# Low-rank token mixing after a block attention: the product over column groups of the array, without a gathering product

## The chip, the cores and the metric

The kernel runs on one core of one Trainium2 chip. The metric is the device time of that core in microseconds (us). The kernel before takes 680.86 us, the median of three executions (679.89 to 681.67). The profiled execution took 680.53 us, of which the page covers a span of 678.7 us, with a mean granted TensorE clock of 0.997.

A core has a matrix engine (TensorE, PE on the page, its weight loads PEld), a vector engine (VectorE, DVE), a scalar engine (ScalarE, ACT), a general engine (GpSimd, POOL) and a queue that issues most transfers (SyncE, SP). Products land in PSUM and are read from there by VectorE or ScalarE.

## The reference, cut to what matters

```python
# attention: 4 batches, 8 heads, 768 positions, 64 channels, in blocks of 64, with decay
intra = ((qb @ kb^T) * Dmask) @ vb
out   = intra + (qb * lam_pow) @ kv_state
kv_state = lam_block * kv_state + (kb * rev_pow)^T @ vb
# heads side by side: x is (4, 768, 512)
h = x^T @ U @ V            # U (768, 32), V (32, 768): mixing over the positions
u = x + h^T
return u + relu(u @ w_ch1) @ w_ch2     # (512, 2048) and (2048, 512)
```

The weights arrive as 64-bit floats, and the kernel takes their two 32-bit words apart itself.

## The kernel before, in words

**Tiles.** The 4 x 768 positions are 24 tiles of 128 rows, six to a batch. The attention works a tile at a time, numbered s from 0. For each tile TensorE turns q and k (`prep`, L353), makes the scores (`scores`, L398), applies the state (`inter`, L439), multiplies masked scores by v (`intra`, L451) and makes the next state's addition (`state`, L416). ScalarE copies the transposes (L356) and the result x (L456) out of PSUM and scales the old state (`fade`, L390). VectorE masks the scores (L407) and adds up the state (L422, L424). GpSimd scales q and k (L381, L370).

**Order.** The order is written out by hand in the list `pieces`. Each engine executes what is meant for it strictly in that order, so an instruction that waits holds all that come after it on its engine. Step s prepares tile s + 1 and finishes tile s. Seven tiles behind, `mix` adds the low-rank part to x (PE L497, DVE L500) and `turn` transposes the sum for the channel products (L514 and after) and writes it out (L517).

**Low-rank part.** Once per batch, h is made in two halves: p = U^T x, of 32 rows and 512 columns, by `low`, and then V^T p by `mix`. Before the change `low` gives each of the first four position tiles a column group of 32 columns of the array, so that four partial sums of p lie one below the other in PSUM (L465). The last two tiles are cut into halves of 256 columns and added to the four (L474). ScalarE copies this out (L479), and `low_sum` multiplies it by a matrix `gather` of ones and noughts (L483), which adds the four parts and writes p four times, once to each group of 32 partitions. Then p is cut into a high part, of which ScalarE writes 64 rows (L489), and a low part, of which VectorE writes 64 rows (L490). `mix` multiplies these 128 rows by v_hl, which holds V cut up to match.

**Weight conversion beside it.** `aside(s)` runs small steps out of a table: the fetches of a weight tile, then `one` (L153, L154, and two ScalarE steps L159 and L160), `two` (L170), `three` (L178), `four` (L183), `five` (L201) and so on. Tile 0 of the first channel weight is fetched in four parts in steps 3 to 6, and `one` comes in step 7. In steps 0 to 6 `aside` stands at the end of a step, from step 7 on it stands in the middle, ahead of the masking of the next tile. U is converted in steps 1 and 2, V in steps 3 to 5.

**Buffers.** There are nine tiles of x (`x_pool`), three raw tiles of q and of v and four of k, two banks pair `px` and `pss`, and single banks by tags such as "pq", "pk", "pt" and "pu". A tag's next tile waits until the last reader of the former is done.

**After the attention** come `hidden` (L708, L718), the first channel product, and then the second (L839, L841, L843). The last tiles of the attention's turning and mixing, and the last batch's low-rank part, are spread among the first products by the list `rest`.

**Start.** `keep_busy` multiplies blank tiles so that TensorE isn't idle before the first data. `constants` makes the mask by scans over the decay factors (L299), and `powers` the decay powers for q (L312).

Of the kernel before, what the change touches and what calls it, by code (L numbers as in the profile page):

```python
# [8 lines left out]
FP32 = mybir.dt.float32  # L9
# [5 lines left out]
P = 128  # L15
# [3 lines left out]
def kernel(  # L19
# [223 lines left out]
    def one_bank(shape, name, tag):  # L243
        return psf.tile(shape, FP32, tag=tag, name=name)
# [4 lines left out]
    def bank(shape, name, tag):  # L249
        return psa[0].tile(shape, FP32, tag=tag, bufs=2, name=name)  # L250
# [31 lines left out]

    gather = keep.tile([P, G, R], FP32, name="gather")
# [11 lines left out]
    def constants():  # L295
        for a in range(HP):
            for x in range(2):
                h = 2 * a + x
                nc.vector.tensor_tensor_scan(  # L299
                    mask[:, x, a, :], lamb[:, h : h + 1].broadcast_to([P, P]), ident, 0.0,  # L300
                    ALU.mult, ALU.add,
                )
        nc.vector.tensor_copy(out=rev, in_=mask[:, :, :, P - 1])
# [12 lines left out]

    def make_gather():
        grid = ident.rearrange("p (g r) -> p r g", r=R)
        nc.vector.tensor_reduce(out=gather[:, 0, :], in_=grid, axis=mybir.AxisListType.X, op=ALU.add)
        for g in range(1, G):  # L320
            nc.vector.tensor_copy(out=gather[:, g, :], in_=gather[:, 0, :])
# [137 lines left out]
    pts = {}  # L459

    def low(b):

        pp = one_bank([P, C], "pp", "pu") if b < B - 1 else bank([P, C], "pp", "b2")
        for c in range(G):
            nc.tensor.matmul(  # L465
                out=pp[c * R : (c + 1) * R, :], lhsT=u_w[:, c, :], rhs=xs[b * NT + c],
                start=True, stop=False,
            )

        n = C // 2  # L470
        assert 2 * (NT - G) == G
        for i in range(G):
            c, cols = G + i // 2, slice(i % 2 * n, (i % 2 + 1) * n)
            nc.tensor.matmul(  # L474
                out=pp[i * R : (i + 1) * R, cols], lhsT=u_w[:, c, :],
                rhs=xs[b * NT + c][:, cols], start=False, stop=True,
            )
        pts[b] = tmp("pt")
        nc.scalar.copy(pts[b], pp)  # L479

    def low_sum(b):
        pr = one_bank([P, C], "pr", "pt") if b < B - 1 else bank([P, C], "pr", "b2")
        nc.tensor.matmul(  # L483
            out=pr, lhsT=gather.rearrange("p g r -> p (g r)"), rhs=pts.pop(b),
            start=True, stop=True,
        )
        t = tmp("pt_h")
        nc.vector.tensor_scalar(t.bitcast(U32), pr.bitcast(U32), HI, None, ALU.bitwise_and)
        nc.scalar.copy(p_hl[0 : P // 2], t[0 : P // 2])  # L489
        nc.vector.tensor_tensor(  # L490
            out=p_hl[P // 2 : P], in0=pr[P // 2 : P], in1=t[P // 2 : P], op=ALU.subtract
        )
# [52 lines left out]
    pieces += [("powers", 0)]  # L545
    for s in range(NS):
# [3 lines left out]
        step = [("low", b - 1)] * (c == 0 and b > 0)  # L550
        step += [("prep", s + 1), ("scale", s + 1)] * more
        step += [("mix", done)] * (0 <= done < NS - NT - 1)
        step += [("low_sum", b - 1)] * (c == 0 and b > 0)
# [10 lines left out]
    def load_next(name, engine=nc.sync):  # L564
# [7 lines left out]
        "low": low, "low_sum": low_sum, "mix": mix, "turn": turn,  # L572
# [45 lines left out]
    for steps, at in (  # L618
        (u_side, (-1, 1, 1, 2, 2)),
        (v_steps(), (0, 0, 3, 3, 4, 4, 5, 5, 5, 5)),  # L620
        (w1_steps(0, True), (3, 4, 5, 6, 7, 8, 9, 10, 12, 13, 14)),
# [33 lines left out]
    make_gather()  # L655
    keep_busy(2)
    pl = one_bank([P, H], "pl", "pt")
    nc.tensor.matmul(out=pl, lhsT=lam_row[:, H:], rhs=lam_row[:, 0:H], start=True, stop=True)
    keep_busy(3)
    nc.vector.tensor_copy(out=lamb, in_=pl)  # L660
    constants()
    scale_k(0)
    run.update(aside=aside, late=on_scalar_late, powers=lambda s: powers())
# [89 lines left out]
    def run_units(units, side, every=lambda i: None):  # L753
# [10 lines left out]
        (0, 4, "turn", c0 - 2), (0, 6, "mix", c0 - 1), (0, 9, "low", b), (0, 14, "low_sum", b),  # L764
# [177 lines left out]
```

## Time and profile before

| view | value |
|---|---|
| median of three | 680.86 us |
| span of the profile | 678.7 us |
| PE busy | 668.4 us (98%) |
| VectorE busy | 495.8 us (73%) |
| ScalarE busy | 291.5 us (43%) |
| GpSimd busy | 114.6 us (17%) |
| share of PE in the chain that ended last | 97% |
| attention, up to its last tile | to 126 us |

The page puts the busy time of each engine beside its share of the span. The chain of work that ended last is followed back from the last instruction, at each step to what released it. A busy engine with a large share of that chain bounds the kernel; where another engine or a transfer stands in the chain, the bound changes for that stretch. The list of waits says who waited for whom, with the sum in us, the number of waits and the longest. A timeline line has the start in us, the length in us, the engine, the line of the code, the operation, output and inputs, and the number of instructions merged. Most of the attention's time passes at one step per tile, which is read between the starts of successive `px` products in the chain: 81.99, 86.73, 91.46 and 96.20 us, so 4.74 us each.

### The profile page before, as it was taken

To read this page: it belongs to the slowest core of one execution; us is meant where nothing else is said; L and a number is where in the kernel's file an instruction comes from. 1 tells how busy PE (TensorE), PEld (TensorE's weight loads), DVE (VectorE), ACT (ScalarE), POOL (GpSimd) and SP (SyncE) were. 2 spreads that over 40 slices of the span, in tenths; PEclk is the share of its full clock that TensorE was granted. 3 is DMA by queue.
4 is the path that set the end of the run, shared out by engine and by line. 5 is a ranking of instruction groups with operands and counts; after the bars stand their busy time and mean duration, and the time that the engine had idled before them with its cause. 6 is when DMAs were issued, how large, how long until landed. Compare 5 with 4: busy or idle time off the path is not lost.

```text
span 678.7 us, 13340 instructions
## 1 busy us (share of the span) xinstructions
PE 668.4 (98%) x5196; PEld 543.0 (80%) x5196; DVE 495.8 (73%) x857; ACT 291.5 (43%) x543; POOL 114.6 (17%) x92
## 2 busy tenths in 40 slices
PE   8979999999999999999999999999999999999997
PEld 7869888778888888888888888888888888888886
DVE  5658899686999777777798255787586676865854
ACT  4657777545665444444465131232232322322320
POOL 4446667331000000000000000030030210300300
PEclk9998999999999999999999999999999999999999
DMA  9898985145677655555566999955363353453421
GB/s 214 196 224 217 223 220 144 64 168 173 234 249 261 233 202 202 205 204 204 204 249 248 330 320 370 312 164 167 95 214 101 108 196 102 152 163 94 158 92 62
DMA packets 131776, 131.29 MB, mean 193 GB/s; under 512 B 81346, under 2 KB 89794, under 8 KB 131714
## 3 DMA queue, kind: packets, MB, share of 16 engines
q1 hardware_dynamic: 130656, 130.18, 60.4%
q8 instruction: 41, 0.67, 0.4%
q10 hardware_dynamic: 1058, 0.26, 0.2%
q14 instruction: 21, 0.17, 0.1%
HBM read 80.09 MB, written 50.33 MB: 192 GB/s over the span
## 4 chain that ended last, share of the span: by engine, by line
PE 97%; DVE 1%; DMA 1%; issue 0%; POOL 0%; SPq 0%; ACT 0%; DVEq 0%; POOLq 0%
PE pz L708 27%; PE pz L841 13%; PE pz L839 13%; PE pd L718 13%; PE pd L843 13%; PE px L451 4%; PE pss L398 4%; PE put L514 2%; PE pq L353 2%; PE pk L353 1%; PE px L439 1%; PE pkv L416 1%; PE pu L497 1%; DMA words<-in_moe_w_ch_dram 1%; PE pp L465 1%; PE pr L483 1%
## 5 line engine op out<-in xcount | busy, mean ns | idle before, releaser
L708 PE MATMUL pz<-u_hl,w 128*128 128x512 f32 x768 | 191.2, 398 | 0.2 <-ACT r L714 0.2
L708 PEld LDWEIGHTS pz<-u_hl,w 128*128 128x128 f32 x768 | 143.9, 188 | 36.4 <-issue 1.1
L839 PE MATMUL pz<-w_hl,m 128*128 128x512 f32 x384 | 151.6, 396 | 0.0
L841 PE MATMUL pz<-w_hl,m 128*128 128x512 f32 x384 | 151.6, 396 | 0.0
L843 PE MATMUL pd<-w_d,m 128*128 128x512 f32 x384 | 150.0, 396 | 0.0
L822 ACT ACTIVATE m<-mt 128x512 fp32r<-128x512 f32 x96 | 60.7, 632 | 195.5 <-PE pd L843 145.6
L823 DVE SCALAR_TENSOR_TENSOR m<-rm,m 128x512 fp32r<-128x512 f32 x96 | 71.5, 746 | 53.9 <-ACT m L822 53.6
L868 POOL TENSOR_TENSOR o<-o,u 128x512 f32<-128x512 f32 x20 | 29.8, 1524 | 447.5 <-DVE o L864 447.5
L723 DVE SCALAR_TENSOR_TENSOR r<-pd,r 128x512 f32<-128x512 f32 x96 | 61.8, 685 | 55.6 <-ACT r L714 41.2
L718 PE MATMUL pd<-u_d,w 128*128 128x512 f32 x384 | 98.2, 397 | 0.0
L841 PEld LDWEIGHTS pz<-w_hl,m 128*128 128x128 f32 x384 | 72.3, 188 | 17.7
L843 PEld LDWEIGHTS pd<-w_d,m 128*128 128x128 f32 x384 | 72.3, 188 | 17.6
L839 PEld LDWEIGHTS pz<-w_hl,m 128*128 128x128 f32 x384 | 72.3, 188 | 17.6
L718 PEld LDWEIGHTS pd<-u_d,w 128*128 128x128 f32 x384 | 72.2, 188 | 17.4
L714 ACT ACTIVATE r<-pz 128x512 f32<-128x512 f32 x96 | 52.0, 593 | 59.0 <-PE pz L708 59.0
L824 DVE SCALAR_TENSOR_TENSOR m<-m 128x512 fp32r<-128x512 f32 x96 | 69.0, 720 | 0.9
L821 DVE TENSOR_SCALAR mt<-rm 128x512 uint32<-128x512 uint32 x96 | 46.2, 481 | 25.8 <-DMA rm<-r_d 25.2
L204 ACT CAST w<-wt 128x512 fp32r<-128x512 f32 x32 | 19.9, 622 | 40.9 <-DVE wt L201 33.7
L407 DVE TENSOR_TENSOR sm<-pss,mask 128x512 f32<-128x512 f32 x48 | 30.8, 682 | 8.6 <-PE pss L398 8.6
L451 PEld LDWEIGHTS px<-vraw,sm 128*64 128x64 f32 x768 | 24.6, 138 | 11.2 <-DVE sm L407 6.4
L451 PE MATMUL px<-vraw,sm 128*64 128x64 f32 x768 | 28.2, 225 | 4.0 <-DVE sm L407 3.9
L381 POOL TENSOR_TENSOR qs<-qt,powq 128x512 f32<-128x512 f32 x20 | 25.8, 1289 | 25.5 <-ACT qt L356 17.2
(88 smaller groups left out, 703.6 us busy)
## 6 DMA issues: line engine op xcount, KB each, us to landing
r_d<-r SPq DMA_DIRECT2D x96, 256.0 KB, 2.4
rm<-r_d SPq DMA_DIRECT2D x96, 256.0 KB, 2.7
words<-in_moe_w_ch_dram SPq DMA_DIRECT2D x30, 512.0 KB, 4.4
w_d<-w SPq DMA_DIRECT2D x16, 768.0 KB, 3.3
w_hl<-w_d SPq DMA_DIRECT2D x16, 512.0 KB, 6.6
vraw<-in_v_dram SPq DMA_DIRECT2D x24, 256.0 KB, 4.1
u_d<-x_nat SPq DMA_DIRECT2D x24, 256.0 KB, 3.6
u<-u_d SPq DMA_DIRECT2D x24, 256.0 KB, 4.0
```

What stands on the lines that cost most here:

```text
L451: nc.tensor.matmul(out=px[half[t], x, a, :], lhsT=sm[:, x, a, half[t]], rhs=vr[:, 2 * a + x, :], start=(first and a == 0), stop=(a == HP - 1),
L708: nc.tensor.matmul(out=acc[g][0], lhsT=w[:, n, ct, :], rhs=uhl[g][:, n, ct, :], start=(ct == 0 and n == 0), stop=(ct == CT - 1 and n == 1),)
L714: nc.scalar.mul(rs[g], acc[g][0], 1.0 + E)
L718: nc.tensor.matmul(out=acc[g][1], lhsT=w[:, 2, ct, :], rhs=ud[g][:, ct, :], start=(ct == 0), stop=(ct == CT - 1),)
L723: nc.vector.scalar_tensor_tensor(rs[g], acc[g][1], 4096.0, rs[g], ALU.mult, ALU.add)
L821: nc.vector.tensor_scalar(t.bitcast(U32), r.bitcast(U32), HI, None, ALU.bitwise_and)
L822: nc.scalar.activation(out=m[:, 0], in_=t, func=AF.Relu)
L823: nc.vector.scalar_tensor_tensor(m[:, 1], r, 0.0, hi, ALU.max, ALU.subtract)
L824: nc.vector.scalar_tensor_tensor(m[:, 2], hi, E, low, ALU.mult, ALU.subtract)
L839: nc.tensor.matmul(out=pz, lhsT=m[:, 0, cols], rhs=hl[:, 0], start=first, stop=False)
L841: nc.tensor.matmul(out=pz, lhsT=m[:, 1, cols], rhs=hl[:, 1], start=False, stop=end)
L843: nc.tensor.matmul(out=pd, lhsT=m[:, 2, cols], rhs=dd, start=first, stop=end)
```

## The change

The change has four parts. `low` gives each column group of the array a quarter of the columns of x rather than a position tile of its own: for each of the six tiles, four products of 32 rows by 128 columns, which add up over the tiles in place. No sum over groups is then left, so `gather`, its product, the ScalarE copy ahead of it and its set-up go. p lies in PSUM as four blocks; `low_rows` puts them side by side with small VectorE instructions, and ScalarE twice and GpSimd once write the copies. `low` moves behind `prep` and `mix` of its step. `one` of weight tile 0, and `two`, `three`, `four` with it, come a step later. At the start two of five blank products go, `powers` moves from behind the first masking to ahead of the first scaling of k, and `rev` is copied after it.

```diff
-        pp = one_bank([P, C], "pp", "pu") if b < B - 1 else bank([P, C], "pp", "b2")
-        for c in range(G):
-            nc.tensor.matmul(
-                out=pp[c * R : (c + 1) * R, :], lhsT=u_w[:, c, :], rhs=xs[b * NT + c],
-                start=True, stop=False,
-            )
...
-        pts[b] = tmp("pt")
-        nc.scalar.copy(pts[b], pp)
-
-    def low_sum(b):
...
+        pp = one_bank([P, P], "pp", "pq") if b < B - 1 else bank([P, P], "pp", "b2")
+        for c in range(NT):
+            for g in range(G):
+                nc.tensor.matmul(
+                    out=pp[g * R : (g + 1) * R, :], lhsT=u_w[:, c, :],
+                    rhs=xs[b * NT + c][:, g * P : (g + 1) * P],
+                    start=(c == 0), stop=(c == NT - 1),
+                )
+        pps[b] = pp
+
+    def low_rows(b):
+
+        pp, t = pps.pop(b), tmp("p_h")[0:R]
+        h, h2, l, l2 = (p_hl[g * R : (g + 1) * R] for g in range(G))
+        own = [(slice(g * R, (g + 1) * R), slice(g * P, (g + 1) * P)) for g in range(G)]
+        for rows, cols in own:
+            nc.vector.tensor_scalar(
+                t[:, cols].bitcast(U32), pp[rows].bitcast(U32), HI, None, ALU.bitwise_and
+            )
+        nc.scalar.copy(h, t)
+        nc.scalar.copy(h2, t)
+        for rows, cols in own:
+            nc.vector.tensor_tensor(
+                out=l[:, cols], in0=pp[rows], in1=t[:, cols], op=ALU.subtract
+            )
+        nc.gpsimd.tensor_copy(out=l2, in_=l.bitcast(FP32))
...
-        step = [("low", b - 1)] * (c == 0 and b > 0)
-        step += [("prep", s + 1), ("scale", s + 1)] * more
+        step = [("prep", s + 1), ("scale", s + 1)] * more
         step += [("mix", done)] * (0 <= done < NS - NT - 1)
-        step += [("low_sum", b - 1)] * (c == 0 and b > 0)
+        step += [("low", b - 1)] * (c == 0 and b > 0)
+        step += [("low_rows", b - 1)] * (c == 0 and b > 0)
...
-        (w1_steps(0, True), (3, 4, 5, 6, 7, 8, 9, 10, 12, 13, 14)),
+        (w1_steps(0, True), (3, 4, 5, 6, 8, 9, 10, 11, 12, 13, 14)),
...
     make_identity(nc, ident)
-    make_gather()
-    keep_busy(2)
+    keep_busy(1)
     pl = one_bank([P, H], "pl", "pt")
     nc.tensor.matmul(out=pl, lhsT=lam_row[:, H:], rhs=lam_row[:, 0:H], start=True, stop=True)
-    keep_busy(3)
+    keep_busy(2)
     nc.vector.tensor_copy(out=lamb, in_=pl)
     constants()
+    powers()
+    nc.vector.tensor_copy(out=rev, in_=mask[:, :, :, P - 1])
     scale_k(0)
...
-        (0, 4, "turn", c0 - 2), (0, 6, "mix", c0 - 1), (0, 9, "low", b), (0, 14, "low_sum", b),
+        (0, 4, "turn", c0 - 2), (0, 6, "mix", c0 - 1), (0, 9, "low", b), (0, 14, "low_rows", b),
```

The list `pieces` also loses its own entry for `powers`.

## The prediction

> **What bounds the kernel.** I read the page first. PE is busy for 668.4 of 678.7 us and is 97% of the chain that ended last, so what the change is worth is what it takes off PE's time line. That is read from the chain in order of time (start us, length us, what):
>
> ```profile
> 9.51 1.38 DVE powq L312 x4
> 11.06 1.25 POOL qs L381
> 12.35 0.69 PE px L439 x32
> ...
> 41.41 1.08 PE px L451 x32
> 42.50 0.59 PE pkv L416 x16
> 43.09 1.02 SPq L267
> 44.16 4.31 DMA words<-in_moe_w_ch_dram
> 49.26 1.21 DVE sm L407 x2
> 50.51 1.04 PE px L451 x28
> 51.55 0.71 PE pkv L416 x16
> 52.26 1.92 PE pss L398 x32
> 54.17 0.85 PE px L439 x32
> ...
> 68.90 1.00 PE pp L465 x8
> ...
> 71.66 0.86 PE pr L483 x2
> ```
>
> Two places aren't PE: the start, and the hole from 43 to 50 us, where the last fetched part of weight tile 0 stands in the chain. The waits up to 260 us and up to 160 us say who stood there (us in total, times, longest):
>
> ```profile
> PE px L451 <- DVE sm L407: 3.9, 2, 3.6
> ```
> ```profile
> DVE sc L153 <- DMA words<-in_moe_w_ch_dram: 4.9, 1, 4.9
> ```
>
> So `one` waits at the head of VectorE's queue for a transfer that lands at 48.5 us (issued 44.16, 4.3 us to landing), the masking of tile 8 is queued behind it, and PE waits for the masking. The table by stretches (PE, PEld, DVE, ACT, POOL busy, granted clock, DMA share, GB/s) shows the aftermath:
>
> ```profile
> 43.00:51.00 8.00, 4.13 (x101) 3.61 (x99) 2.92 (x6) 2.27 (x7) 2.48 (x3) 1.00 0.92 218
> 51.00:56.00 5.00, 5.00 (x109) 4.76 (x104) 4.61 (x8) 3.92 (x9) 2.75 (x2) 0.66 0.93 240
> 77.00:96.00 19.00, 19.00 (x502) 17.45 (x500) 18.09 (x30) 15.92 (x37) 15.38 (x12) 1.00 0.90 225
> ```
>
> PE worked 4.13 of 8 us and then ran at clock 0.66. In the ordinary stretch PE is full, but VectorE is busy for 18.1 of 19 us and the DMA engines for 0.90: both stand close behind PE.
>
> **What the Trainium skill says.** *TensorE: Matmul & The Clock Gate*, "What's actually happening": after an idle window of about 3.4 us the array falls to half its clock and needs such a window of work to get back. The trace agrees: after the 3.6 us wait the scores took 1.92 us against 1.03. *TensorEngine Tiling (Array Packing)*, "Key Properties": the four 128x32 tiles load and multiply in parallel. The trace agrees: eight L465 products of 604 ns each are over in 1.06 us. *GPSIMD Engine Reference*, "Specifications": GpSimd shares its SBUF interfaces with VectorE, and two-input or two-port VectorE instructions contend. The trace fits: L201 took 0.99 us at 74.57 beside GpSimd work, 0.43 in the median.
>
> **1. `one` a step later.** The hole: `px` starts at 41.41 and, two tiles on, at 56.73, 15.32 us; two ordinary steps are 9.47. It costs 5.85 us, the wait and the slow clock together. After the change `one` stands in step 8. VectorE reached it at 43.6 us and will reach the new place an ordinary step later, at about 48.3; the part lands at 48.5, if SP keeps its times (its issues there run some 4 us behind the program because the DMA engines are full, not because PE is late). The wait is some 0.2 us. Behind it stands the masking of tile 9, with 0.5 us to spare before PE wants it. I take 5.8 us of gain; bounds 4.5 and 5.85.
>
> Moved with it: `two`, `three` and `four` to steps 9 to 11. VectorE's ordinary step is masking 1.29, turning 1.36, mixing 0.68, state 0.42, so 3.75 us, and the largest of these conversions 1.29 (L170): 5.04 against 4.74, 0.3 over for a single step, absorbed in the next. Nothing.
>
> **2. The start.** The chain runs powq, qs, then the first state product at 12.35. `powers` (1.75 us from 9.14 to 10.89) moves to before the first masking, where VectorE waited 2.06 us for the scores. k's scaling starts 1.7 us later, and ends 8.6 instead of 7.0 for tile 0, wanted by PE at 10.1: hidden. qs of tile 1 then waits for GpSimd's second scaling, at about 9.7, and ends at 11.0; the product is then free after the scores, at 11.8. With 0.3 us from fewer blanks (first q lands at 3.1, PE turned it at 4.48) this is 0.5 to 0.8 us early. But v of tile 4, issued at 22.53, lands at 26.26, and its product starts at 26.60: of the gain 0.34 gets through. I take 0.3; bounds 0 and 0.6.
>
> **3. The low-rank product on PE.** Before, from first L465 to the next transpose: 68.83 to 70.26, 1.43 us, and `pr` 0.86 in the chain. New: 24 products, 48 records as an fp32 product has two, four groups at once, so 12 rounds of 128 columns. The nearest row is L398, four small tiles at once with 128 columns: 32 records in 1.03, so 0.129 a round, and 1.55 us. From L465's 0.43 per 512 columns it would be 0.108 a round plus 0.2 of drain, 1.5. The weight loads, four in 0.13 us at L474, just keep up. PE saves 1.43 + 0.86 - 1.55 = 0.74 us a batch, and 0.1 more where a change of shape is saved. Bounds: 1.5 and, with loads and products in turn, 12 x 0.26 = 3.1.
>
> **4. `low_rows` beside it.** It takes eight VectorE instructions of 32x128 from PSUM. Rows: 256 columns 0.42, 512 columns 0.69, so 0.29 for 128; successive ones overlap by 0.06, so 0.23, 1.85 us in all. *VectorE: DVE Perf Modes*, "The TRN2 errata", gives 120 + 128 cycles, an estimate of 0.26. Against two instructions of 0.69 this is 0.45 more, in three of 24 steps. ScalarE: two casts of about 0.6 (L489 0.62) against a copy and a cast, equal, but both now stand ahead of the copy of x (L456), and `inter` of the next tile wants that bank. By batch:
> - Steps 12 and 18. `low` ends at 71.67; four ANDs to 72.7; the casts to 73.95; x to 74.5. PE wants `inter` at 74.25: 0.3 lost of 0.85. 0.5 gained each.
> - Step 6. V's conversion is in the way: VectorE is in it until 36.5, ScalarE writes V's copies for 2.08 us (L599), both ahead of the first `mix`. Following them: ANDs 37.4, casts 38.6, x 39.15, V's copies 41.15, `mix` 41.2 against 40.9 before. Also `low` waits some 0.4 us for the "pq" bank it now shares. 0.3 us lost; bounds -0.8 and +0.5.
> - Last batch, among the channel products: nothing there waits on x, `mix` is 13 instructions away. 0.75 gained.
> GpSimd's copy (L370, two inputs, takes 1.06 for 512) ends at about 75, `mix` wants it at 76.5: hidden.
>
> **5. What the DMA engines ask back.** A step moves q, k, v and the written sum, 1.05 MB, and 0.13 of weights in steps 8 to 11: 1.18 MB, 4.9 us at the highest rate seen, 240 GB/s, against 4.74. In the hole SP caught up its 4 us; now it won't. q, k, v have 8 us to spare. The nine x tiles have less: tile s takes the buffer of s - 9, whose write is issued at the end of step s - 2. From there to the copy are 6.9 us, and landing takes about 4: at 4 us behind, x is 1 us late, 0.75 us of which hides behind `state` and `scores`. I take 0.6 us in all; bounds 0 and 3.
>
> **Sum.** 5.8 + 0.3 + 0.5 + 0.5 - 0.3 + 0.75 - 0.6 = 6.95 us. Behind 126 us PE is full to the end, so it comes through: 680.86 - 6.95 = **673.9 us**.
>
> **Rivals.**
> - *The DMA engines take the hole's place.* For it: share 0.92 to 0.95 from 30 to 56 us. Against: buffers for three tiles. Half the hole comes back: 5.85/2 less, so 676.8.
> - *The row work holds PE.* For it: VectorE and ScalarE are nearly full in steps 12 and 18. Against: they had 0.7 us of idle time there. Each batch loses 0.5 instead of its gain (1.45 in sum): 3.45 us less, 677.4.
> - *Slower: the column groups don't overlap.* 48 records in turn at 0.129 are 6.2 us instead of 2.29: 3.9 us x 4 lost, 15.6, against 6.1 of points 1 and 2: 690.4. Against it: L465 overlaps by four.
>
> **Chances.** Forecast 0.66 (672.6 to 675.2), DMA 0.18, row work 0.09, slower 0.05, nothing gained 0.02. The range takes in the first two and part of the third: 672.3 to 677.2. The bound of 0.3% is 2.04 us, 678.8: faster 0.91, same 0.04, slower 0.05.
>
> **What would show it.** The wait of L153 for words falls from 4.9 us to under 0.6, with no stretch at clock 0.66; PE is busy for nearly all of 43 to 51 us. The 48 low records of a batch span about 1.55 us. In step 12 `inter` waits for ScalarE. Tile 1's `px` L439 starts before 12 us. I am wrong if `one` waits again, if ScalarE's copies of x wait for transfers by several us, or if the low records span over 3 us.

## The result, and the profile after

The changed kernel took 679.79 us in the median of four executions (679.27 to 680.83), beside 680.38 us for the kernel before (679.10 to 681.67). The ratio is 0.9993, with a 95% interval from 0.9970 to 1.0017. So the forecast of 673.9 us missed: a gain of 6.95 us was expected, and 0.5 us was measured, which can't be told from none.

Yet the wait that was to go has gone. The page says so first, in its shares of busy time and in the shares of the chain that ended last:

```profile
PE 666.0 (98%) x5312; PEld 544.2 (80%) x5312; DVE 499.2 (74%) x877; ACT 291.7 (43%) x543; POOL 116.4 (17%) x96
...
PE 93%; ACT 2%; DVE 1%; issue 1%; DMA 1%; POOL 0%; SPq 0%; ACTq 0%; DVEq 0%
```

No wait of L153 for `words` is left in the list of waits. But PE's share of the chain fell from 97% to 93%: other engines took its place on the path. The table by stretches has the same windows as before the change (PE, PEld, DVE, ACT, POOL busy, granted clock, DMA share, GB/s):

```profile
43.00:51.00 8.00, 6.82 (x169) 5.73 (x170) 4.29 (x7) 4.95 (x15) 3.38 (x3) 1.00 0.96 229
51.00:56.00 5.00, 4.52 (x113) 3.91 (x109) 4.52 (x6) 3.60 (x9) 3.91 (x4) 1.00 0.92 238
77.00:96.00 19.00, 18.36 (x491) 16.96 (x486) 16.83 (x28) 15.11 (x36) 14.77 (x12) 1.00 0.84 208
```

In the stretch of the hole PE is busy for 6.82 us instead of 4.13, and the clock stays at 1.00. But the third window was full before, 19.00 of 19, and has lost 0.64. The chain in order of time shows who stands in these places (start us, length us, what):

```profile
39.40 0.62 ACT vp L473
40.04 0.62 ACT vp L474
40.68 0.58 ACT x_nat L447
41.68 0.51 ACT vp L585
...
42.77 0.49 issue
43.51 0.81 ACT faded L381 x3
...
45.33 0.69 PE pkv L407 x16
...
51.82 0.97 DVE sc L153
52.79 1.42 DVE m L154
54.21 1.21 DVE sm L398 x2
55.46 1.06 PE px L442 x28
...
58.17 0.63 ACT sc L159
58.82 0.72 ACT sc L160
...
61.50 0.69 PE pkv L407 x16
...
84.04 0.64 issue
84.68 0.57 PE px L430 x23
```

Four things are to be seen. Around 40 us ScalarE's casts of the row work and V's copies hold the fading, and with it PE. At 52 us `one` is on the path without waiting for anything: L153 and L154 alone take 2.39 us ahead of the masking. At 58 us its exponents (L159, L160) stand on ScalarE ahead of the copies that PE wants. And at 84 us PE stops for 0.64 us with no wait at all.

A plainer measure is used below: the length of a step, from the start of the intra product of one tile to that of the next, read from the trace of each kernel. An ordinary step is 4.74 us. Step 8 is the one that ends with the product of tile 8. (The program's step s runs on past the product of tile s, so what it does last lies in the table's step s + 1.) "px 23" is when tile 23's product starts, counted from the start of the span, and "rest" is from there to the end. These are single executions, so sizes are taken from the ratios of many runs, and places from here. They differ from their start on: the product of tile 5 begins at 30.80 us before, at 32.45 after, and between 29.8 and 33.5 us in all traces, so a late tile 23 isn't by itself a loss of the edit. (The rows of e3, e5, e13, e14 and e16 are left out.)

```
step                7     8     9    10    11    12    13    14    18    19    px 23   rest
before             5.11  8.57  6.74  4.74  4.73  6.32  4.73  4.74  6.32  4.74  125.21  553.49
after              5.86  6.48  5.12  5.25  5.19  5.39  5.80  4.74  5.39  5.88  125.77  553.03
e0_before_again    5.01  7.48  5.25  5.19  4.97  6.32  4.74  4.73  6.32  4.74  124.81  553.49
e1_shift           4.38  5.58  5.19  5.26  5.18  6.32  4.74  4.73  6.32  4.74  121.02  553.48
e2_shift_low       5.84  5.88  5.12  5.25  5.18  5.39  5.80  4.74  5.39  5.95  124.01  552.79
e4_low             5.25  5.88  4.74  5.36  4.84  5.39  5.80  4.74  5.39  5.95  125.00  552.80
e6_rows_split      5.37  5.87  5.12  5.26  5.19  5.39  4.78  5.35  5.39  5.74  123.87  552.83
e7_spread          4.84  5.88  4.74  4.73  5.10  6.33  4.73  4.74  6.72  4.74  121.61  553.49
e10_split_spread   5.36  5.87  5.15  5.11  5.74  6.89  5.05  5.08  6.66  5.20  126.28  552.82
e8_before_three_v  4.30  5.50  4.74  5.23  4.97  6.32  4.74  4.73  6.32  4.73  121.68  553.32
e9_shift_three_v   4.37  5.58  5.18  5.26  5.19  6.32  4.74  4.73  6.32  4.73  121.39  553.31
e11_after_three_v  5.85  5.87  5.13  5.26  5.18  5.39  5.99  4.74  5.39  5.80  121.97  552.83
e12_split_three_v  5.37  5.87  5.13  5.26  5.18  5.39  4.78  5.08  5.39  5.05  120.38  552.62
e15_spread_three_v 5.04  5.87  4.73  4.94  4.93  5.39  5.05  5.08  6.65  5.05  122.06  552.64
```

(Steps 12 and 18 hold the low-rank product, and with it are longer than the ordinary one. Step 8 isn't an ordinary one either: in the sixteen traces without the hole, the changed kernel's aside, it takes 5.50 to 5.94 us.)

### The profile page after: what moved, and what is told of

It reads as the page before. It is cut to its first block, busy times and chain, and to the rows that moved or that the text cites. A ratio compares the mean times of both kernels' runs of the same rounds, so it can differ in the third digit from the quotient of the medians.

```text
span 678.8 us, 13604 instructions
## 1 busy us (share of the span) xinstructions
PE 666.0 (98%) x5312; PEld 544.2 (80%) x5312; DVE 499.2 (74%) x877; ACT 291.7 (43%) x543; POOL 116.4 (17%) x96
## 4 chain that ended last, share of the span: by engine, by line
PE 93%; ACT 2%; DVE 1%; issue 1%; DMA 1%; POOL 0%; SPq 0%; ACTq 0%; DVEq 0%
PE pz L695 27%; PE pz L826 13%; PE pz L828 13%; PE pd L705 13%; PE pd L830 13%; PE pss L389 3%; PE px L442 3%; PE put L501 2%; PE pq L344 1%; PE pk L344 1%; PE px L430 1%; PE pkv L407 1%; PE pp L457 1%; PE pu L484 1%; DMA kraw<-in_k_dram 1%
## 5 line engine op out<-in xcount | busy, mean ns | idle before, releaser
L389 PE MATMUL pss<-qt,kt 64*64 64x128 f32 x768 | 28.6, 282 | 1.1 <-issue 1.1
L159 ACT ACTIVATE sc<-sc,ends 128x512 f32<-128x512 uint32 x30 | 21.7, 722 | 18.4 <-DVE sc L153 18.4
```

What stands on the lines that cost most here:

```text
L389: nc.tensor.matmul(out=pss[half[t], x, a, :], lhsT=kt[half[x], a, half[t]], rhs=qt[half[x], a, :], start=True, stop=True,)
```

## The experiments

Every kernel was run beside the kernel before, in five groups on four chips. The median of the kernel before was 677.94 us in group a, 679.40 in b, 679.83 in c, 678.65 in d and 679.66 in e, so the table has ratios. Within a group they compare directly. Across groups the kernel before alone moved by 0.28%, and no run shows that another kernel moves with it; so where two groups are compared the difference of the medians in us stands beside that of the ratios, and what the two don't agree on isn't shown.

| kernel | what it is | group | median us | ratio to before | 95% interval |
|---|---|---|---|---|---|
| after | the changed kernel | own | 679.79 | 0.9993 | 0.9970 to 1.0017 |
| e0_before_again | the kernel before, unchanged | b | 680.00 | 1.0000 | 0.9980 to 1.0020 |
| e1_shift | before + later conversion | a | 677.18 | 0.9985 | 0.9969 to 1.0001 |
| e3_shift_start | e1 + the new start | a | 677.63 | 0.9986 | 0.9972 to 1.0000 |
| e4_low | before + new low-rank part | a | 678.51 | 0.9998 | 0.9975 to 1.0020 |
| e2_shift_low | e1 + new low-rank part | a | 678.56 | 1.0008 | 0.9987 to 1.0028 |
| e5_five_blanks | after + all five blanks | b | 678.44 | 0.9986 | 0.9974 to 0.9998 |
| e6_rows_split | e2 with the row work split | b | 676.94 | 0.9953 | 0.9937 to 0.9968 |
| e7_spread | conversion two steps later | b | 676.96 | 0.9964 | 0.9950 to 0.9978 |
| e8_before_three_v | before, v fetched for 3 tiles | c | 676.09 | 0.9942 | 0.9922 to 0.9962 |
| e9_shift_three_v | e1, v fetched for 3 tiles | c | 676.58 | 0.9946 | 0.9926 to 0.9966 |
| e11_after_three_v | after, v fetched for 3 tiles | d | 677.94 | 0.9986 | 0.9968 to 1.0004 |
| e12_split_three_v | e6, v fetched for 3 tiles | d | 675.51 | 0.9957 | 0.9941 to 0.9974 |
| e10_split_spread | e6 and e7 together | c | 678.93 | 0.9984 | 0.9973 to 0.9995 |
| e15_spread_three_v | e10, v fetched for 3 tiles | e | 676.34 | 0.9938 | 0.9914 to 0.9962 |
| e16_later_fetch | e10, tile 1's parts fetched later | e | 679.22 | 0.9991 | 0.9976 to 1.0005 |
| e13_spread_pt | e10, product in another bank | d | 678.98 | 1.0003 | 0.9988 to 1.0019 |
| e14_split_pt | e6, product in another bank | d | 679.58 | 1.0007 | 0.9994 to 1.0021 |

### The parts alone: conversion, start, low-rank product

**e1_shift**, the conversion alone:

```diff
-        (w1_steps(0, True), (3, 4, 5, 6, 7, 8, 9, 10, 12, 13, 14)),
+        (w1_steps(0, True), (3, 4, 5, 6, 8, 9, 10, 11, 12, 13, 14)),
```

> The kernel before with the conversion of weight tile 0 a step later, and nothing else. Theory A (each part does what it does alone, and the later step is worth nearly the whole hole at 43 us, while the row work and the colder array at the start give it back): 4.0 to 5.8 us faster than the kernel before, that is 674.6 to 676.4. Theory B (the hole was the DMA engines' rest; taken away, what it hid comes out as waits for late loads and late instructions): 1 to 3 us faster, 677.4 to 679.4, with PE idle spread over the steps after 50 us.

Measured: 0.9985, so 1.0 us of gain (0 to 2.1, hardly to be told from none), where the hole alone was to give 5.8. Step 8 is 5.58 instead of 8.57. But steps 8 to 11 sum to 21.21 us, 2.25 over four ordinary ones. Of these 0.84 are step 8's, which is over at 46.27 us, before `one` begins. The other 1.41 lie in steps 9 to 11. VectorE's instructions in order of time show the first part of them (start us, length us, what, idle before):

```profile
48.35 1.03 DVE L153 TENSOR_SCALAR sc<-words 128x512 uint32<-128x512 uint32 x1
49.30 1.50 DVE L154 TENSOR_SCALAR m<-words 128x512 uint32<-128x512 uint32 x1
50.73 1.27 DVE L407 TENSOR_TENSOR sm<-pss,mask 128x512 f32<-128x512 f32 x2
51.92 0.68 DVE L519 TENSOR_SCALAR ut<-put 128x512 uint32<-128x512 uint32 x1
```

`one` finds its words there: no idle time stands in brackets. It takes 2.38 us from 48.35 to 50.73, and the masking behind it is late. From there the chain of e1 goes through ScalarE, where the exponents (54.76 to 56.13 us) stand ahead of the copies of q and k. PE's waits from 40 to 66 us name the masking and the copy of k:

```profile
PE pkv L416 <- ACT kt L356: 0.8, 2, 0.6
PE px L451 <- DVE sm L407: 0.6, 2, 0.4
```

Of the 0.8 us for the copy of k, 0.6 are at 42 us, in step 8 and ahead of `one`; 0.2 are at 58 us, behind the exponents.

**e3_shift_start** adds the new start to it:

```diff
-    keep_busy(2)
+    keep_busy(1)
...
-    keep_busy(3)
+    keep_busy(2)
...
+    powers()
+    nc.vector.tensor_copy(out=rev, in_=mask[:, :, :, P - 1])
     scale_k(0)
```

> The changed kernel with the low-rank part as before, its gathering product included. Theory A: the row work loses 0.3, 0.1 and 0.1 us in the first three batches and gains 0.76 in the last, so it comes out even, 679.4 to 680.2. My prediction's sizes (0.5 gained in two batches, 0.75 in the last, 0.3 lost in one) would make this 1.45 us slower than the changed kernel, 681.2.

Measured: 0.9986 beside 0.9985. The start gave nothing and cost nothing that can be told.

**e4_low**, the new low-rank part alone (product, row work, order of the steps, no gathering product), and **e2_shift_low**, with the later conversion as well (e4 with the diff of e1):

> The kernel before with the new low-rank part alone. The hole at 43 us ends when the weight part lands, whatever PE lost ahead of it, so the first batch's loss is hidden in both theories. Theory A: 0.76 gained in the last batch, 0.1 lost in each of the two in between: 0.5 us faster than before, 679.9. The prediction's sizes: 1.75 us faster, 678.6.

> The changed kernel with the start as before (five blank products, the powers behind the first masking). Theory A: the start costs 1.0 to 1.7 us in the changed kernel, so this takes 678.1 to 678.8 against its 679.8. Theory B: the loads set the pace up to 30 us whatever the start does, so within 0.4 us of the changed kernel.

Measured: 0.9998 and 1.0008. In e4's trace the product of tile 7 starts at 44.27 us, 2.97 later than before, and yet that of tile 8 starts at 50.15, within 0.28 us of the 49.87 of before. Most of the 2.97 isn't the low-rank part's, as tile 5, ahead of it, was 2.67 late already. But it shows what the hole does: when PE comes late, the part has landed (L153 waits 0.2 us for it and not 4.9, and PE doesn't wait for the masking), so what goes wrong ahead of it costs next to nothing. In e2 the hole is gone, and nothing takes up the loss of steps 6 and 7. Ratio by ratio the low-rank part cost 0.0023 (1.6 us) on top of e1, 1.4 us between the medians; the two intervals overlap.

### The start again, and the kernel before again

**e0_before_again** changes nothing.

> The kernel before, unchanged, for a second profile. Theory C (the hole's end is set by when the DMA engines deliver the last part of weight tile 0, and that differs between executions by several us; the profile I predicted from showed a long one): the part is issued nearer to 42 than to 44 us, the hole between the px products of tiles 7 and 9 costs 2 to 4 us over two ordinary steps rather than 5.85, and the span is shorter by the same. Theory A (the hole is a fixed property of the program): 5.5 to 6 us again. Its time against itself shows what a comparison of this kernel can tell: 1.000 within 0.0015.

Measured: 1.0000. Its trace holds a smaller hole:

```profile
DVE sc L153 <- DMA words<-in_moe_w_ch_dram: 3.8, 1, 3.8
```

3.8 us instead of 4.9; PE stood idle for 2.62 us, not 3.61, and no slow clock followed, so step 9 is 5.25 and not 6.74. Steps 8 and 9 are 12.73 us, so the hole costs 3.26 us here and cost 5.84 in the first trace. Tile 8's product starts at 49.88 and 49.87 us in the two, although tile 7's starts are 1.10 us apart: the end of the hole stands fast, as L153 begins when the part has landed, at 48.48 and 48.50 us.

How often the long hole comes can be estimated from the mean granted clock of each execution. It was 0.997 in the trace of before, with its stretch at 0.66, and 0.999 in this one. Of the 225 executions of the kernel before in the five groups, 79 have 0.997 or less, and these take 2.1 to 2.7 us longer than the others of their group (medians). Of the 200 executions of the ten kernels with a later conversion and all of v, three have. So the slow clock seems to follow the hole in about a third of the executions. The other 44 of the kernel before in group a have a median of 677.52 us, beside 677.18 for e1: by the medians about half of what e1 gains is that this slow clock no longer comes.

**e5_five_blanks** is the changed kernel with `keep_busy(2)` and `keep_busy(3)` as before.

> The changed kernel with the five blank products of the kernel before, its powers still ahead of the first scaling. If the missing blanks leave the array at its low clock up to 10 us: scores of tile 0 back from 1.99 us to some 1.5, transposes of tile 1 from 1.1 to 0.66, and px of tile 0 about 1.0 us earlier, of which at most 0.4 us is left in the time, since v of tile 4 sets a floor at 26 us: 679.4 to 679.8 against the changed kernel's 679.8 of its own comparison. If the loads alone set the early pace: no change in the slope, and px of tile 0 within 0.2 us.

Measured: 0.9986, beside 0.9993 for the changed kernel itself, whose interval holds it. In its trace the scores of tile 0 take 1.59 us (1.99 in the changed kernel); but with five blanks as well they took 1.50 in the trace of before, 1.98 in e0_before_again and 1.99 in e1_shift. So the clock at the start differs between executions of one kernel, and the blanks aren't shown to decide it.

### Row work and conversion mended

**e6_rows_split** takes e2_shift_low and splits `low_rows`, so that the copy of x stands ahead of the casts on ScalarE, and the state's addition ahead of the subtractions on VectorE:

```diff
-        step += [("low_rows", b - 1)] * (c == 0 and b > 0)
-        step += [("intra", s)] + [("late", s)] * (done < 0) + [("state", s)]
+        new = c == 0 and b > 0
+        step += [("rows_and", b - 1)] * new + [("intra", s)] + [("rows_high", b - 1)] * new
+        step += [("late", s)] * (done < 0) + [("state", s)] + [("rows_low", b - 1)] * new
```

> The kernel with the later conversion and the new low-rank part, start as before, but with the row work taken apart: the four ANDs first, then the copy of x ahead of ScalarE's two casts, and the addition of the state ahead of VectorE's four subtractions. If the row work holds PE by standing ahead of these two: the step of tile 13 and 19 falls from 5.80 and 5.95 to 4.8 to 5.1, that of tile 7 by 0.5, and the kernel becomes 1.5 to 2.2 us faster than with the row work in one piece (678.6), 676.4 to 677.1. If something else holds PE there (GpSimd's scaling, the mode change of the array): less than 0.4 us.

Measured: 0.9953 (0.9937 to 0.9968), 3.2 us under before. In its own group it is 0.0033 under e5, the changed kernel with five blanks (1.5 us between the medians); under e2_shift_low, in another group, it is 0.0055 by the ratios and 1.6 us by the medians. So it is faster than the kernel before and than the changed one. The lines show why. ScalarE in the changed kernel, step 12:

```profile
72.22 0.62 ACT L473 CAST vp<-p_h 32x512 fp32r<-32x512 f32 x1 [2.54 <-DVE p_h L470]
72.85 0.62 ACT L474 CAST vp<-p_h 32x512 fp32r<-32x512 f32 x1
73.49 0.58 ACT L447 COPY x_nat<-px 128x512 f32<-128x512 f32 x1
```

The copy of x waits behind two casts, which waited 2.54 us for VectorE. `inter` wants the bank that this copy frees. PE's line for it:

```profile
74.18 0.69 PE L430 MATMUL px<-kv,qs 64*64 64x64 f32 x32 [0.83 <-POOL vp L479]
```

The profile puts the 0.83 us down to GpSimd's L479. But `inter` starts 0.11 us after the copy of x ends (73.49 + 0.58), it needs nothing of L479, and with the order turned round the wait is gone: step 13 falls from 5.80 to 4.78. It was the copy. (The trace of e6 as a whole doesn't show the gain: it lost 1.7 us to stops without a wait, see e12, and took 678.47 us, 1.5 over its median.)

**e7_spread** is the kernel before with the conversion of tile 0 two steps later, and that of tile 1 one step later:

```diff
-        (w1_steps(0, True), (3, 4, 5, 6, 7, 8, 9, 10, 12, 13, 14)),
-        (w1_steps(1, True), (8, 9, 10, 11, 15, 16, 17, 18, 19, 20, 21)),
+        (w1_steps(0, True), (3, 4, 5, 6, 9, 10, 11, 12, 13, 14, 15)),
+        (w1_steps(1, True), (8, 9, 10, 11, 16, 17, 18, 19, 20, 21, 22)),
```

> The kernel before with the conversion of weight tile 0 two steps later instead of one (steps 9 to 15), and tile 1's one step later (16 to 22), so that one conversion step falls in each step. If the 2.25 us that came back in the steps of tiles 8 to 11 are VectorE's and ScalarE's backlog from the conversion (L153 and L154 took 2.4 us beside GpSimd, the exponents 1.4 us on ScalarE): the later place, where the backlog of V's copies is gone, gives 0.7 to 1.3 us of it back, 675.9 to 676.5 against 677.2 with one step. If the DMA engines set the pace of these steps: no change, 677.2.

Measured: 0.9964 (0.9950 to 0.9978), 2.4 us under before. VectorE's lines for `one`:

```profile
54.27 0.43 DVE L153 TENSOR_SCALAR sc<-words 128x512 uint32<-128x512 uint32 x1
54.62 0.41 DVE L154 TENSOR_SCALAR m<-words 128x512 uint32<-128x512 uint32 x1
```

L153 and L154 take 0.43 and 0.41 us here, and 1.03 and 1.50 in e1_shift, and steps 9 and 10 are ordinary ones again. So their time depends on where they stand. GpSimd's lines beside them, in e1 and in e7:

```profile
48.04 1.06 POOL L370 TENSOR_TENSOR ks<-kraw,small 128x512 f32<-128x512 f32 x1 [0.32 <-POOL qs L381]
49.05 1.46 POOL L536 TENSOR_TENSOR u_d<-te,u_hl 128x512 fp32r<-128x512 f32 x1
```

```profile
54.58 1.59 POOL L536 TENSOR_TENSOR u_d<-te,u_hl 128x512 fp32r<-128x512 f32 x1 [0.95 <-ACT te L534]
```

In e1 L153 ends 0.28 us after the first of them, and L154 0.29 us after the second. The other traces agree. In the twelve in which GpSimd's scaling of k was running when L153 began, L153 took 0.78 to 1.03 us and ended 0.28 to 0.29 us after it. In six (before, e7, e10, e13, e15, e16) nothing ran on GpSimd when L153 began; there the two took 0.41 to 0.44 us each, although in four of them GpSimd's u_d ran beside L154. So an instruction of GpSimd that is there first seems to hold VectorE's until it is done, rather than both being slowed. This fits the shared SBUF interfaces that the prediction names; it is read from the order of the times, as no run took GpSimd's work away.

### The transfers taken away

Five kernels (e15 further down) fetch v for their first three tiles only, and leave out the fetches of the other 21:

```diff
+        if name == "v" and s >= 3:
+            raw[s, name] = kept[s % 3]
+            return
...
+        if name == "v":
+            kept[s] = t
```

> The kernel before, but v is fetched for the first three tiles only and those three buffers are used again for all later tiles (the output is not the reference's). A tile then moves a quarter less, some 0.79 instead of 1.05 MB, in the same time. Theory A (the hole is the DMA engines' backlog: the weight part is issued 4 us late because the engines are full): the part is issued when the program asks for it, L153 doesn't wait for it, the step of tile 8 falls from 8.57 us (before) or 7.48 (the same kernel again) to under 5.3, tile 9's too, and the run is 3.3 to 5.8 us shorter than before: ratio 0.991 to 0.995. The gaps that PE shows with no wait, once in some 253 records, become shorter as well. Theory B (the part is issued late because SP or the program's order holds it, not the engines): L153 still waits 3 us or more and the ratio is within 0.998 to 1.002.

**e8** measured 0.9942 (0.9922 to 0.9962), 3.9 us under before, with no wait for `words` in its list, while `one` is still in step 7. Step 8 is 5.50, where under 5.3 was expected. So the hole was the backlog of the transfers and not the place of `one`. The edit both lightens the DMA engines and takes v's issues off SP's queue, where they took 2.1 to 2.7 us each from 37 to 48 us in the trace of before; it doesn't part the two.

> The same cut of v's transfers, on the kernel with the later conversion alone (the output is not the reference's). If the 2.25 us that tiles 8 to 11 lose there are the conversion's own (VectorE beside GpSimd, ScalarE's exponents) and not the transfers', the steps of tiles 8 to 11 stay at 5.2 to 5.6 us, so that this kernel gains only 0 to 2 us on the same kernel with all of v, and ends beside or behind the kernel before with v cut: ratio 0.992 to 0.998. If the full DMA engines cause them, these steps fall to 4.75, and it is some 2.2 us faster than with all of v: ratio 0.993 to 0.996, with the steps telling the two apart.

**e9** measured 0.9946, the same as e8: where there is no hole, moving `one` is worth nothing. And its steps 8 to 11 are 5.58, 5.18, 5.26 and 5.19, those of e1 with all of v to 0.01 us. What the conversion loses at its new place is its own and not the transfers'. (Beside e1, in another group, e9 is 0.0039 ahead by the ratios but 0.6 us by the medians, and the steps show no place for a gain.)

> The changed kernel, with v fetched for its first three tiles only (the output is not the reference's). Theory A (the loss with the new low-rank part is the engines' own: row work ahead of the copy of x, the conversion beside GpSimd): tiles 12 to 14 and 18 to 20 keep what they lose, tiles 8 to 11 too, and the kernel ends behind the one before with v cut (0.9942): ratio 0.994 to 0.998. Theory B (the transfers take it: late k at the start, late instructions, late x): the forecast's gains appear, 1.4 us below the kernel with the later conversion and v cut (0.9946): ratio 0.990 to 0.993.

**e11** measured 0.9986, just beyond the upper end of theory A and far from theory B: with the transfers out of the way the changed kernel is still behind e9, which has the old low-rank part and start, by 0.0040 (2.7 us) in the ratios and 1.4 us in the medians of the two groups. PE's waits from 60 to 126 us are one line, the copy of x again under GpSimd's name, in steps 13 and 19:

```profile
PE px L435 <- POOL vp L484: 1.7, 2, 0.8
```

> The kernel with the row work split and the start of before, with v fetched for its first three tiles only (the output is not the reference's). Without the transfers' load the gaps of PE that show no wait (0.54, 0.26 and 0.74 us in tiles 14 to 19 with all of v) should go, if a full DMA engine delays what PE fetches: then these steps fall to 4.74 and the ratio is 0.991 to 0.993. If they stay, they belong to the number of PE's instructions and not to the load: ratio about 0.995.

**e12** measured 0.9957, 2.0 us under e11 in the same group, so the split row work pays without the transfers' load as well. On the gaps without a wait it is half an answer. In the trace of e6_rows_split they are all that PE waited for from 60 to 126 us:

```profile
PE px L431 <- issue: 1.7, 4, 0.7
```

In e12's trace there is no such line, nor in those of e8, e9, e11 and e15 for that stretch. So with lighter transfers the gaps go. What they cost in a typical execution of e6 stays open: the ratio is no better (0.9957 beside 0.9953), the median is 1.4 us lower in another group, and the traced execution of e6 took 678.47 us, where its median is 676.94.

### Both repairs together

**e10_split_spread** is e6 with the conversion of e7.

> The changed kernel with the start of before, the row work split around the copy of x and the state addition, and the conversion another step later (steps 9 to 12; tile 1's 16 to 18 and so on). If the two repairs act on separate losses they add: the split was worth 0.0055 of the time against the same kernel without it, the spread 0.0021 against the kernel with the conversion one step later alone. So 0.9953 - 0.0021: ratio 0.993 (0.9915 to 0.9945), 4.8 us under before. If both only make room for the same wait (VectorE's and ScalarE's backlog in steps 8 to 12), the ratio stays at 0.9953. The steps of tiles 9 and 10 should be at 4.8, that of tile 13 under 5.

Measured: 0.9984. The repairs don't add; together they are worth less than each alone, by 0.0031 and 0.0020 in the ratios and 2.0 us in the medians. ScalarE's copies of x in steps 9, 10 and 11 tell of a wait that was in neither kernel (in brackets the idle time before, and its releaser):

```profile
54.92 0.59 ACT L448 COPY x_nat<-px 128x512 f32<-128x512 f32 x1 [1.54 <-DMA u_d<-x_nat]
60.67 0.59 ACT L448 COPY x_nat<-px 128x512 f32<-128x512 f32 x1 [2.17 <-DMA u_d<-x_nat]
66.95 0.59 ACT L448 COPY x_nat<-px 128x512 f32<-128x512 f32 x1 [2.32 <-PE pq L345]
```

A copy of x has to wait until the tile nine before has been written out of the same buffer. The writes were issued at 49.49, 55.43 and 61.29 us, and writes landed up to 5.4 us after issue in this stretch. That reaches to the first two copies. The third, which the profile puts down to PE though its product had been running since 63.67, would fit as well; the landing of its write isn't in the trace. Behind the copy on ScalarE stands that of q, and the low-rank product takes the bank that q's copy frees:

```profile
69.11 1.08 PE L458 MATMUL pp<-x_nat,u_w 128*32 128x128 f32 x32 [1.57 <-ACT qt L348]
```

> The kernel with both repairs, with v fetched for its first three tiles only (the output is not the reference's). If the transfers made the repairs cancel, ScalarE's copies of x no longer wait for the writes of x (1.5, 2.2 and 2.3 us), the low product no longer waits for the bank of q (1.57 and 0.85), tiles 12 and 18 fall to 5.4 us and tile 23 starts by 131.5 us (137.81 with all of v): ratio 0.991 to 0.995, ahead of the split alone with v cut (0.9957). If ScalarE and VectorE are out of time by themselves, the waits for the bank stay and the ratio is 0.997 to 0.999.

(That text counts tile 23 from the trace's own start, 11.2 to 11.5 us ahead of the span: 131.5 there is 120.3 here, and 137.81 is 126.28.)

**e15** measured 0.9938 (0.9914 to 0.9962). The copies of x wait for their products alone, and step 12 is 5.39. So the late copies of x were the transfers' doing. That they are all that made the repairs cancel isn't shown. Beside the split alone with v cut, e12 in another group, e15 is ahead by the ratios (0.9938 and 0.9957) but 0.8 us behind by the medians, and its tile 23 starts at 122.06 and not at 120.3, where e12's starts at 120.38. The second wait for q's bank, 0.85 us in step 18, stays with v cut, so that one isn't the transfers'.

> The kernel with both repairs, where the four parts of weight tile 1 are fetched in steps 12 to 15 and not 8 to 11, so that the writes of x no longer stand behind a part on SP's queue and a step moves 1.05 instead of 1.18 MB there. If the late writes of x made the repairs cancel, the copies of x in steps 9 to 11 wait for the products alone and the ratio is 0.993 to 0.996. If not, it stays at 0.998. A risk: the last part now lands for a conversion one step later, in step 16, where the hole of before could come back (3 us): ratio then 1.0.

**e16** moves tile 1's four fetches from steps 8 to 11 to steps 12 to 15. In its trace the copies of x no longer wait for writes, and step 12 is 5.39. But the ratio is 0.9991 (0.9976 to 1.0005): a miss, 0.0053 behind e15 in the same group. The waits of the copies can go without a gain. `one` of tile 1 waited 0.5 us for its words, step 17 grew to 5.83, and its executions lie between 676.75 and 682.97 us; the traced one took 677.90. What the slower ones wait for isn't in a trace. It stays open.

> The kernel with the row work split and the conversion spread, where the product of the low-rank part takes the PSUM bank of the turned tiles (freed by VectorE's subtraction) and not that of q (freed by ScalarE's copy). If the shared bank made the two repairs cancel, the waits before the product (1.57 us in step 12, 0.85 in step 18) go, tiles 12 and 18 fall from 6.89 and 6.66 to some 5.4, and the ratio from 0.9984 to 0.994 or below. If VectorE and ScalarE are simply out of time in these steps, the wait moves to another bank or to the masking, the steps of tiles 11 to 14 keep their sum (24.8 us against 23.7 with the split alone), and the ratio stays at 0.998.

> The kernel with the row work split alone (0.9953), with the product in the bank of the turned tiles. It waited 0.3 us in step 6 and 0.4 in step 12 for q's bank, so at most 0.7 us are to be had: ratio 0.9943 to 0.9953. If VectorE's subtraction frees the other bank later than ScalarE frees q's, it is slower: 0.996 or more.

**e13** and **e14** give the product the bank of the turned tiles. They measured 1.0003 and 1.0007. Beside the same kernels with q's bank, in other groups, e14 is behind by 0.0054 and by 2.6 us between the medians, and e13 by 0.0019 but level in the medians (678.98 and 678.93). The wait moved from ScalarE to VectorE. PE's line in e13:

```profile
PE pp L458 <- DVE u_hl L530: 2.4, 2, 1.3
```

So for the split alone q's bank was the better one, and the shared bank alone doesn't explain e10, which stays open in part.

## Why the prediction was wrong, point by point

**Step 1, the hole: wrong in size, and in what it was.** That `one` would find its part, that PE would be busy in the stretch and the clock stay up, came true. The term of 5.8 us is what failed: alone it measured 1.0 (0 to 2.1), in e1. There are four reasons. First, the 5.85 us were read from one execution with a long hole and the slow clock after it; the next trace of the same kernel had 3.26, and by the clocks of all executions only about a third seem to have the slow stretch. The Trainium skill's page *TensorE: Matmul & The Clock Gate*, "What's actually happening", fits both: 3.61 us idle brought the slow clock, 2.62 did not, on either side of its 3.4. Second, they were counted over two ordinary steps, and step 8 isn't one: without the hole it takes 5.50 us or more in every trace, in e7 as well, where `one` comes two steps later. So 0.76 us or more of it was never to be had. Third, the hole was a sink. Its end stood at 49.87 and 49.88 us although PE came to it 1.10 us apart (e0), and in e4 PE came 2.97 us late and went on only 0.28 us late; taking the hole away also made real whatever is lost ahead of it. Fourth, "`two`, `three` and `four`: nothing" was wrong. That reckoning priced one VectorE instruction at 1.29 us, and left out that `one` itself could take 2.4 us, and that its exponents (0.63 and 0.72 on the path at ScalarE) stand ahead of the copies of q and k. Steps 9 to 11 give back 1.41 us in e1 and in e9, and 0.35 in e7.

**Step 2, the start: 0.3 forecast, nothing found** (0.9986 beside 0.9985). In the trace of the changed kernel tile 1's `px` L430 starts at 12.67 us, so the sign that was to show it is missing. In e5's it starts at 11.72, as foreseen, but with the start of before it is at 11.89 and 11.91 in e2 and e7, so the sign doesn't tell the two starts apart.

**Step 3, the product on PE: right.** The row for it reads

```profile
69.24 1.32 PE pp L457 x41
```

in the chain, and the whole 48 records span 1.52 us, where 1.55 was forecast. The column groups overlap. In the last batch, where nothing waits behind it, "rest" falls from 553.49 to 552.79 in e2 and 552.80 in e4: 0.7 us, with 0.75 forecast.

**Step 4, the row work: the mechanism right, the size wrong, and that decided it.** The prediction had the casts ahead of the copy of x and took 0.3 us for it. It forecast 1.85 us for the eight VectorE instructions, as successive ones would overlap:

```profile
70.90 1.23 DVE L470 TENSOR_SCALAR p_h<-pp 32x128 uint32<-32x128 uint32 x4
72.16 1.24 DVE L476 TENSOR_TENSOR vp<-pp,p_h 32x128 fp32r<-32x128 f32 x4
```

They took 2.47, 0.31 each. The estimate of 0.26 from the Trainium skill's page *VectorE: DVE Perf Modes*, "The TRN2 errata", would have been short as well, but nearer than 0.23. Ahead of the copy of x stand only the four ANDs, 1.23 us where 1.03 was taken. The other part of the error is the way from one engine to the next, which the sum left out: 0.14 us from the end of the product to the first AND, 0.09 from the ANDs to the first cast, 0.11 from the copy of x to `inter`. So the wait of `inter` became 0.83 us and not 0.3. Steps 12 and 13 together are 11.19 us instead of 11.06: a loss of 0.13 where 0.5 was to be gained, and 0.21 lost in steps 18 and 19. In step 6 more may be lost: from tile 5's product to tile 7's are 10.8 us in all five traces with the row work in one piece and 10.32 in e6. With the old part they are 9.81 in e1 and 9.80 in e9, 10.54 before, and 11.31 and 11.03 in e0 and e3. So between 0.3 and 1.0 us is lost against e1, e9 and the first trace, where 0.3 was forecast with 0.5 as its bound. The chain above shows how, with the casts, x and V's copies one behind the other on ScalarE from 39 to 43 us. The rival "the row work holds PE" named this with 0.09, for 677.4 us. That it was the main loss of the new part is shown by the split: within a group it brought 0.0033 of the time back in e6 against e5, and 0.0029 in e12 against e11, some 2 us each.

**Step 5, the transfers: 0.6 us in one form, several in others.** The forecast looked at late x. The changed kernel shows no copy of x waiting for a write; e10 does, 1.5 to 2.3 us each, where the other waits had been cleared. And e8 shows that cutting the transfers is worth 3.9 us to the kernel before, the most that any one edit gave to it. The rival "the DMA engines take the hole's place", with 0.18, was near to the truth in kind, but it gave them half the hole, and at this place it was step 8 itself and the conversion that took the rest.

So step 1's term, sized at 5.8, and step 4's, sized at a gain, are where the forecast failed. The sum of 6.95 became 1.0 from the conversion, about 0 from the start, and a loss of 0.5 to 1.6 from the low-rank part (0.9986 to 0.9993 with the new start, 0.9985 to 1.0008 with the old one); the intervals, some 0.0015 to 0.002 to each side, do not part these further. The 680.86 us that the forecast set out from were the median of three executions; the medians of the groups, of 225 in all, are 677.94 to 679.83.

## What to carry to other kernels

A wait for a transfer that arrives at a fixed time hides every loss ahead of it: before its length is counted as a gain, ask what else becomes visible when it is gone, read its length in more than one execution, and count it against the step as it is without the wait. When small work is moved, price every engine that it touches, and above all what its instructions stand ahead of in each queue; here the order of three instructions on ScalarE and VectorE was worth more than the whole change. Where two engines and the transfers are all close to full, repairs need not add, and each has to be measured with the others in place.

## What the runs showed of the hardware

PE stops with no wait that the profile shows ("issue"). The page has a queue that moves instructions, in packets of some 16 KB; this is its line after the change:

```profile
q8 instruction: 42, 0.69, 0.4%
```

That is 42 packets beside 10624 records of products and weight loads, and 41 beside 10392 before: some 253 records to a packet. The stops lie 252 to 254 records apart, or two or three times as many (in e6 at records 3719, 3973, 4225 and 4731, in e13 at 3217, 3975 and 4227). A step of these kernels has 250 records from tile 8 on, so a stop that belonged to a place in the step would come back after 250. From 60 to 126 us all of them fall within the products of `inter`, whose 64 records take 0.46 us.

From 60 to 126 us PE lost 0.3 to 1.9 us to them in eight of the nine kernels with the new product and all of v, and nothing in the five with the old product, nor in the five with v cut. Ahead of 60 us kernels with the old product have them too (0.8 and 0.4 us in e0). A reason may be that with the new product the first step of a batch has 250 records like the others, so that the end of a packet stays in `inter` from step to step, while with the old one it has 190 and the end moves elsewhere. That PE waits there for its own instructions behind the data is what all this suggests; no run delayed them on purpose.

The other surprise is the pair of VectorE instructions of `one`, which took 0.4 us each in one step and 1.0 and 1.5 us in the step before it, ending 0.28 to 0.29 us after the instruction of GpSimd that had been there first.
